# Nine matmuls into an unread PSUM bank, placed in TensorE's last waits for the values of a decode attention kernel

## The chip, the cores and the metric

The kernel runs on one core of a Trainium2 chip. The metric is the device time of one execution in microseconds, as the median of several. One execution per kernel is also recorded by the profiler; the profile's span is some 1.9 us shorter than the device time. The traces of before and after note 16 marks for each of the end's ten transfers, and the landing is taken as the last of them (value part 1 of before: 1264.21 to 1266.39 us); in before the matmuls that wait for one started 0.04 to 0.14 us after it.

## The reference

One token goes through a cached attention and a gated feed-forward; both are added to the input.

```python
xn = layernorm(x)                                      # x: (1, 1, 448)
q  = (xn @ wq).reshape(1, 1, 16, 256)                  # 16 query heads, 8 key/value heads
scores = einsum("bhqd,bhkd->bhqk", q, k) * 256**-0.5   # caches: (1, 8, 65536, 256), bf16
o  = einsum("bhqk,bhkd->bhqd", softmax(scores), v)
out = x + o.reshape(1, 1, 4096) @ wo + ffn(xn)         # ffn(xn) = xn + sigmoid(xn @ w_r) * gated feed-forward of xn
```

The two caches are 537 MB of the 549 MB that the kernel reads.

## The kernel before

The key and value blocks stream through three slots of SBUF. TensorE transposes keys, forms scores, and multiplies probabilities with values. Only the end matters here. The last value block (128 rows for each partition) arrives in six parts, so that little work is left after each landing; behind it, in the same queue of transfers, come the last pieces of the output weights.

```python
LAST = [64, 32, 16, 8, 4, 4]     # rows of the last value block in each part
DIRECT = 2                       # the last two parts are multiplied another way
...
slot_item("v", NT + 3, 2, [("last%d" % k if k < len(LAST) - 1 else "slot2", J) for k, J in enumerate(LAST)], [("SUM",)])
item("wx", [(wo_x, wo_rows(HL, HL + 1)[:, 0, FO // 2:FO, :]...)], [("HT",)])
ENDS = [(0, 0, NH), (1, 0, 1), (1, 1, NH)]
for k, (i, f0, f1) in enumerate(ENDS):
    item(("wo_end", k), [...])   # three more pieces of the output weights
```

The multiplication with the values, part by part. Four matmuls run side by side, each on a strip of 32 columns of the array (`tile_position=(0, 32 * g)`); in the trace of before the four of a group start within 0.01 us (part 1: 1266.530 to 1266.540):

```python
def pe_V(t, c, first, last, loose=False):
    ...
    for k, (_, J) in enumerate(parts):
        ...
        W_item("pe", ("v", t, k))                      # wait for the landing of part k
        def f(it, ...):
            if direct:                                 # parts 4 and 5: two moving columns each
                ...
            for j in range(lo, hi, 2):
                g = j // 2 % NG
                ins = mm(ps_o[32 * g:32 * g + 2 * rep, :],
                         lhsT=p_sb[:, c, j - c * CH:j - c * CH + 2, :]..., rhs=kv[:, j:j + 2, :],
                         start=..., stop=..., tile_position=(0, 32 * g), skip_group_check=loose)
            return ins
        O("pe", ("PV", t, c, k), f)
```

And what follows the values:

```python
values(NT + 3)               # the six parts
dve_ob(T); pe_oT(T)          # VectorE copies the sums out; TensorE regroups; VectorE normalises (OTSB)
W_item("pe", "wx")
O("pe", "FIN_X", fin_x)      # 4 matmuls of 224 columns
W("pe", "OTSB", T)
for k, (i, f0, f1) in enumerate(ENDS):
    W_item("pe", ("wo_end", k))
    O("pe", ("FIN", k), f)   # 4, then 2, then 2 matmuls of 224 columns
W("dve", "FIN", len(ENDS) - 1)
O("dve", "RESULT", ...)      # copy to bf16; two small transfers write it out
```

## Time and profile before

| | before |
|---|---|
| time, median of three runs | 1277.72 us (1277.71 to 1278.37) |
| span of the profiled run | 1275.8 us |
| read from HBM | 549.03 MB at 430 GB/s |
| TensorE matmul busy | 956.0 us, 75% |
| mean granted TensorE clock | 0.897 |
| last landing to copy of the result (trace) | 0.501 us |

The prediction shows the page, the chain, TensorE's instructions and the stretches of the clock. In the trace of before the granted clock is 0.50 or 1.00 throughout, and it changes only at steps that lie a multiple of 3.41 us apart (near the end at 1241.22, 1254.88, 1261.70, 1265.12 and 1268.53); a window of the clock is here a stretch of 3.41 us between such steps. In the timelines below a line has start us, length us, engine, source line, operation, output and inputs, shapes, count, and in brackets the idle time before and what ended it. A timeline merges neighbours, so the length of a merged line includes the waits inside it.

### The profile page before, as it was taken

Reading aid. Unit: us, or ns where it says so; the run is one execution under the profiler, and the core shown is the slowest. Engines: PE = TensorE matmul, PEld = TensorE weight load, DVE = VectorE, ACT = ScalarE, POOL = GpSimd, SP = SyncE. Lnnn points to the kernel's source line nnn. Section 1 sums busy time; section 2 is a strip of 40 time slices with the busy share of each in tenths; the row PEclk is TensorE's granted clock in tenths of the full one; section 3 lists DMA queues with packets and bytes.
Section 4 is the critical chain, followed back from the end, with each engine's and each line's share of the span. In section 5 each row is a group of like instructions: output and inputs, shape, how many; then the busy total and the mean of one; then the engine's idle time right before and its main releaser. Section 6 shows DMA issues by size and latency. Waiting matters only on the chain.

```text
span 1275.8 us, 23503 instructions
## 1 busy us (share of the span) xinstructions
PE 956.0 (75%) x9735; PEld 624.7 (49%) x9735; DVE 570.3 (45%) x1078; ACT 436.2 (34%) x655; POOL 8.0 (1%) x38
## 2 busy tenths in 40 slices
PE   3898988778777679767778776787777687677664
PEld 3676655445544455444455454454454454444321
DVE  4566554345444455343454344454444554444310
ACT  2455433244333334323333332343332333332300
POOL 2000000000000000000000000000000000000000
PEclk9899999899888899888898888898888998888886
DMA  9999999999999999999999999999999999999998
GB/s 408 426 429 443 432 436 432 434 432 438 434 429 438 427 440 429 436 436 429 438 432 436 432 434 427 440 432 434 438 427 438 432 436 434 432 432 436 426 431 353
DMA packets 12742, 549.20 MB, mean 430 GB/s; under 512 B 1335, under 2 KB 1978, under 8 KB 3386
## 3 DMA queue, kind: packets, MB, share of 16 engines
q1 hardware_dynamic: 12724, 549.03, 99.7%
q8 instruction: 8, 0.13, 0.0%
q14 instruction: 4, 0.03, 0.0%
q10 hardware_dynamic: 6, 0.00, 0.0%
HBM read 549.03 MB, written 0.00 MB: 430 GB/s over the span
## 4 chain that ended last, share of the span: by engine, by line
DMA 80%; PE 17%; issue 1%; ACT 1%; DVE 1%; SPq 0%; ACTq 0%; DVEq 0%
DMA ring<-in_A_v_cache_dram 68%; PE ps_o L420 12%; DMA ring<-in_A_k_cache_dram 7%; DMA kt_all<-in_A_wo_dram 3%; DMA ring<-in_A_wo_dram 2%; PE ps_t L420 2%; PE ps_q L420 1%; PE ps_m L420 1%; ACT kt_all L481 1%; SPq L910 0%; DVE kt_all L479 0%; ACT S_sb L562 0%; PE ps_s L420 0%; DVE kt_all L712 0%; DVE kt_all L815 0%
## 5 line engine op out<-in xcount | busy, mean ns | idle before, releaser
L420 PE MATMUL ps_t<-ident_f,ring 128*128 128x128 f32 x4096 | 586.6, 285 | 84.5 <-DMA ring<-in_A_k_cache_dram 61.6
L479 DVE COPY kt_all<-ps_t 128x1024 bf16<-128x1024 bf16 x768 | 487.0, 684 | 293.8 <-PE ps_q L420 289.0
L420 PEld LDWEIGHTS ps_t<-ident_f,ring 128*128 128x128 f32 x4096 | 450.2, 143 | 237.2 <-issue 135.2
L481 ACT ACTIVATE kt_all<-ps_t 128x1024 bf16<-128x1024 bf16 x256 | 262.0, 1023 | 508.4 <-PE ps_q L420 508.4
L420 PE MATMUL ps_o<-ring,p_sb 128*4 128x512 bf16 x2044 | 177.1, 508 | 204.6 <-DMA ring<-in_A_v_cache_dram 200.3
L420 PEld LDWEIGHTS ps_o<-ring,p_sb 128*4 128x4 bf16 x2044 | 53.0, 101 | 292.6 <-issue 264.2
L420 PE MATMUL ps_q<-kt_all,q_cur 128*2 128x512 bf16 x2056 | 164.9, 398 | 0.3 <-DVE kt_all L479 0.3
L503 ACT ACTIVATE s<-ps_q 98x512 bf16<-98x512 f32 x257 | 151.6, 590 | 1.3 <-PE ps_q L420 1.3
L585 DVE RECIPROCAL rs<-ps_m 128x4 f32<-128x4 f32 x29 | 5.3, 182 | 272.2 <-PE ps_m L420 272.2
L572 ACT ACTIVATE p_sb<-S_sb 128x128 bf16<-128x128 bf16 x64 | 18.9, 307 | 260.8 <-PE ps_o L420 260.6
L420 PEld LDWEIGHTS ps_s<-sel_bf,s 128*128 128x128 bf16 x1032 | 64.7, 98 | 5.3 <-ACT s L503 1.9
L420 PE MATMUL ps_s<-sel_bf,s 128*128 128x8 bf16 x1032 | 63.7, 167 | 1.3 <-ACT s L503 1.3
L628 DVE CAST ob_sb<-ps_o 100x512 bf16<-100x512 f32 x29 | 20.0, 691 | 89.9 <-PE ps_o L420 89.9
L420 PEld LDWEIGHTS ps_q<-kt_all,q_cur 128*2 128x2 bf16 x2056 | 26.4, 79 | 44.2 <-issue 44.2
L420 PEld LDWEIGHTS ps_m<-rowsum,ones_f 128*128 128x128 f32 x58 | 12.3, 264 | 22.6 <-issue 22.6
L481 ACT ACT_TABLE_LOAD x7 | 9.0, 1283 | 20.8 <-PE ps_q L420 20.8
L532 DVE TENSOR_REDUCE m1p<-S_sb (+1 forms) x33 | 13.9, 422 | 4.4
L420 PE MATMUL ps_m<-rowsum,ones_f 128*128 128x4 f32 x58 | 14.8, 326 | 0.0
L530 DVE CAST S_sb<-ps_s 128x256 f32 (+1 forms) x33 | 13.6, 413 | 1.9 <-PE ps_s L420 1.9
L562 ACT ACTIVATE S_sb<-S_sb,negmax 128x512 bf16<-128x512 bf16 x16 | 13.2, 851 | 3.2 <-DVE negmax L556 3.2
L420 PE MATMUL ps_m<-diag,ones_f 2*128 2x2 f32 x58 | 11.2, 260 | 3.6 <-DVE diag L547 0.6
L420 PEld LDWEIGHTS ps_m<-diag,ones_f 2*128 2x128 f32 x58 | 8.7, 187 | 10.5 <-DVE diag L547 10.5
(93 smaller groups left out, 128.3 us busy)
## 6 DMA issues: line engine op xcount, KB each, us to landing
ring<-in_A_k_cache_dram SPq DMA_DIRECT2D x8, 4096.0 KB, 30.5
ring<-in_A_v_cache_dram SPq DMA_DIRECT2D x1, 4096.0 KB, 27.3
ring<-in_A_wq_dram SPq DMA_DIRECT2D x1, 3584.0 KB, 11.5
ring<-in_A_wo_dram SPq DMA_DIRECT2D x1, 2688.0 KB, 28.7
ring<-in_A_v_cache_dram SPq DMA_DIRECT2D x1, 2048.0 KB, 31.8
ring<-in_B_w_gate_dram SPq DMA_DIRECT2D x1, 1568.0 KB, 16.5
ring<-in_B_w_up_dram SPq DMA_DIRECT2D x1, 1568.0 KB, 19.9
ring<-in_B_w_down_dram SPq DMA_DIRECT2D x1, 1568.0 KB
```

The source lines that it names most:

```text
L420: return pe.matmul(*a, **k)
L479: O(e, ("EV", s, m), lambda it: nc.vector.tensor_copy(out=kt[:, :], in_=tb[:, :]), f"ev{m}")
L481: O(e, ("EV", s, m), lambda it: nc.scalar.activation(out=kt[:, :], in_=tb[:, :], func=ACTF.Copy), f"ev{m}")
L503: O("act", ("EVQ", s), lambda it: nc.scalar.activation(out=s2[s % 2][0:QROWS, :], in_=ps_q[0:QROWS, :], func=ACTF.Copy), "evq")
L530: O("dve", ("SCOPY", u), lambda it: nc.vector.tensor_copy(out=S_sb[:, at(it, SBN), :], in_=ps_sn), "sc")
L532: O("dve", ("SMAX", u), lambda it: nc.vector.tensor_reduce(out=m1p[:, :, at(it, 1)], in_=S_sb[:, at(it, SBN), :].rearrange("p n i -> p i n ...
L562: O("act", ("EXP", h, i), lambda it, i=i: nc.scalar.activation(out=S_sb[:, :, i], in_=S_sb[:, :, i], func=ACTF.Exp, bias=negmax[:, i:i + 1 ...
L572: O("act", ("PC", t, c), lambda it: nc.scalar.activation(out=p_sb[:, c, :, :], in_=S_sb[:, n:n + CH, :], func=ACTF.Copy), "pc")
L585: O("dve", ("RS", t), lambda it: nc.vector.reciprocal(out=rs[:, :, :], in_=ps_m[0:P, C_TOT:C_TOT + NH * rep]))
L628: O("dve", ("OB", t), lambda it: nc.vector.tensor_copy(out=ob_sb[0:OROWS, :], in_=ps_o[0:OROWS, :]))
```

## The change

In the profile before, TensorE waits in the end for one small part after another, and its granted clock is at half (0.50) from 1268.53 us on. The change fills these waits with matmuls on stale data, and is meant to keep the clock up until the last steps. Their results go to a PSUM bank that nobody reads any more.

```diff
+WARM = {0: (5, 512), 1: (2, 512), 2: (1, 512), 3: (1, 256)}
...
             O("pe", ("PV", t, c, k), f)
+            if t == NT + 3 and k in WARM:
+
+                def keep(it, k=k):
+                    n_, cols = WARM[k]
+                    for _ in range(n_):
+                        ins = mm(ps_tf[3][0:2 * rep, 0:cols], lhsT=p_sb[:, c, 0:2, :].rearrange("p n i -> p (n i)"), rhs=slots[0][:, 0:cols],
+                                 start=True, stop=True, skip_group_check=True)
+                    return ins
+
+                O("pe", ("WARM", k), keep)
```

## The prediction

> **What bounds the kernel now.** I read the page first, then the chain that ended last, then TensorE's instructions of the last 15 us, then the trace's landing marks of the last transfers, and last the busy time cut along the granted clock's own steps. The page:
>
> ```profile
> PEclk9899999899888899888898888898888998888886
> DMA  9999999999999999999999999999999999999998
> ...
> DMA 80%; PE 17%; issue 1%; ACT 1%; DVE 1%; SPq 0%; ACTq 0%; DVEq 0%
> ```
>
> The DMA engines are busy at 90% or more in 39 of 40 slices and the kernel reads 549.03 MB at 430 GB/s, which is 1276.8 us against a span of 1275.8: the kernel is its transfers. The change leaves all of them as they are. Only what follows the last transfer can move. In the same page the clock row falls to 6 in the last slice, which is the mark that the change aims at. The chain that ended last, from the moment when the last transfers are queued:
>
> ```profile
> 1237.23 34.86 DMA kt_all<-in_A_wo_dram
> 1272.09 0.04 issue
> 1272.13 0.54 PE ps_s L420 x4
> 1272.67 0.08 issue
> 1272.74 0.93 PE ps_s L420 x8
> 1273.67 0.02 issue
> 1273.70 0.38 DVE kt_all L862
> ```
>
> On its face TensorE holds the end for 1.47 us (0.54 + 0.93) after a landing at 1272.09. Here are its instructions in the waits for the parts of the last value block (64, 32, 16, 8, 4, 4 rows) and after them:
>
> ```profile
> 1261.64 3.57 PE L420 MATMUL ps_o<-ring,p_sb 128*4 128x512 bf16 x32 [4.66 <-DMA ring<-in_A_v_cache_dram]
> 1266.53 1.03 PE L420 MATMUL ps_o<-ring,p_sb 128*4 128x512 bf16 x16 [1.32 <-DMA ring<-in_A_v_cache_dram]
> 1268.92 1.02 PE L420 MATMUL ps_o<-ring,p_sb 128*4 128x512 bf16 x8 [1.36 <-DMA ring<-in_A_v_cache_dram]
> 1270.21 0.60 PE L420 MATMUL ps_o<-ring,p_sb 128*4 128x512 bf16 x4 [0.26 <-DMA ring<-in_A_v_cache_dram]
> ```
>
> Sixteen matmuls took 1.03 us and then eight took 1.02: the clock fell between them. The aligned stretches show where (columns: stretch and length, then PE, PEld, DVE, ACT, POOL busy us with counts, granted clock, DMA share, GB/s):
>
> ```profile
> 1254.88:1258.29 3.41, 2.10 (x40) 0.72 (x32) 0.00 (x0) 0.62 (x2) 0.00 (x0) 1.00 1.00 428
> 1258.29:1261.70 3.41, 0.06 (x4) 0.09 (x8) 0.00 (x0) 0.00 (x0) 0.00 (x0) 1.00 0.96 408
> 1261.70:1265.12 3.42, 3.42 (x32) 0.95 (x31) 0.00 (x0) 0.00 (x0) 0.00 (x0) 0.50 0.95 402
> 1265.12:1268.53 3.41, 1.12 (x20) 0.32 (x16) 0.00 (x0) 0.00 (x0) 0.00 (x0) 1.00 0.99 403
> 1268.53:1271.94 3.41, 2.38 (x32) 0.88 (x32) 0.69 (x1) 0.00 (x0) 0.00 (x0) 0.50 0.92 336
> 1271.94:1275.36 3.42, 1.54 (x16) 0.38 (x13) 0.54 (x2) 0.00 (x0) 0.00 (x0) 0.50 0.05 15
> ```
>
> The clock of each stretch was decided by the stretch before: 3.42 us busy raised it, 2.10 us kept it, 1.12 and 0.06 us dropped it, and 2.38 us at the low clock did not raise it. So the whole end, from 1268.53 on, ran at half clock.
>
> The last step is the one that decides my number. The trace's landing marks (a transfer has landed with its sixteenth mark) stand at 1266.39, 1268.88, 1270.17, 1270.85 and 1271.51 for value parts 1 to 5, and at 1272.09, 1272.61, 1272.90 and 1273.20 for the four last pieces of the output weights. Each matmul group of the end starts at its own piece: the weight load of the last group is at 1273.24, 0.04 after the last landing. So the 1.47 us that the chain puts down to TensorE are nearly all waiting for four landings in a row; what TensorE alone owns is from 1273.24 to the end of the last pair of matmuls at 1273.65.
>
> [...]
>
> **The change part by part.** It adds nine matmuls of four weight columns: five of 512 after part 0, two of 512 after part 1, one of 512 after part 2, one of 256 after part 3. They write a score-transpose bank whose last reader was the FFN, so nobody waits for the result, and the vector engine's copy of the sums waits for part 3's own matmuls, ahead of the added one.
> - Cost of one, full clock: groups of four side by side start 0.215 us apart, and the added ones all use one column strip, so about 0.215 us each for 512 and 0.107 for 256. At half clock twice that.
> - After part 0: its last group starts at 1264.55 and streams 0.43 us at half clock, so the added five start near 1264.98; the clock rises at 1265.12; they stream until about 1266.12[...]. Part 1 lands at 1266.39. [...]
> - After part 1: its last group starts at 1267.18; two more end streaming near 1267.82; part 2 lands at 1268.88. No delay.
> - The stretch 1265.12 to 1268.53 now has 1.12 + some 1.0 + 0.43 = 2.6 us busy against 1.12, above the 2.10 that kept the clock. So it stays full past 1268.53. This is the step that I am surest of.
> - Part 2 then takes about 0.6 instead of 1.02 us, one added 0.215 us; part 3 about 0.38 instead of 0.60, one added 0.107 us, done near 1270.7; part 4 lands at 1270.85. No delay. The vector copy of 0.69 us starts some 0.2 us earlier, at about 1270.65.
> - Parts 4 and 5 and the regrouping are two-column matmuls [...]about 26 ns apart; they start at their landings and gain next to nothing.
> - The normalised sums (now ready at 1272.23) come perhaps 0.1 us earlier; the next matmul needs the piece of 1272.61. No gain.
> - The last pair: start held by the landing of 1273.20, so 1273.24 to 1273.26 either way. Its 391 ns (median of the eight 224-column matmuls) [...]if the clock is still full there.
>
> That last condition is open. Stretch 1268.53 to 1271.94 would hold about 0.60 + 0.22 + 0.38 + 0.11 = 1.3 us of wide matmuls and some 0.9 us of two-column ones. By busy time that is 2.2 us, on the side that keeps the clock; counting the wide ones alone it is 1.3, close to the 1.12 that lost it. I give it about an even chance, and in other executions the windows lie elsewhere. Sum: 0.13 us times about one half, 0.05 to 0.1 us off 1277.72.
>
> **Rivals.**
> 1. The chain at face value: 12 matmuls of 224 columns and the steps before them run at twice the rate, 0.5 to 0.8 us gained, time near 1277.0. For it: the chain names PE for 1.47 us and the clock is 0.50. Against: four landing marks inside that stretch.
> 2. The added matmuls run at half clock (other window position) and delay the next part: five take 2.13 us instead of 1.08, part 1 starts about 0.9 us late, and up to 0.4 us of this could reach the end; time near 1278.1. [...]Against: TensorE is busy without a break from 1261.64, so a full window lies behind it soon, and the waits later on (1.1 us before part 2) take up most.
> 3. The clock falls again at 1271.94: gain 0, time 1277.7.
> 4. TensorE's extra reads slow the transfers, which would count over the whole wait. Against: GB/s was 402 in the stretch with TensorE busy throughout and 408 in the idle one before it, no difference that tells.
>
> **Range and chances.** The three runs of before spread over 0.66 us (1277.71 to 1278.37), five times the gain that I expect, so the spread sets the range. Predicted 1277.6 us; 8 times in 10 between 1276.9 and 1278.6. A change of 2% would be 25 us, and everything after the last landing is about 2.6 us (1273.20 to 1275.8), so faster or slower by over 2% has half a percent each.
>
> **What would show it right or wrong.** Right: clock 1.00 past the window that ended at 1268.53 here, the eight matmuls of part 2 in about 0.6 us, unchanged landings, and the last pair still starting 0.04 to 0.06 us after the last landing[...]. Wrong: the matmuls on the last four pieces starting well before those landings (then rival 1), a part starting late after added matmuls (rival 2), or the last landing itself moved by more than 0.3 us, for which I know no reason.

Cut from it is what rested on figures that no trace or run of this case shows, or named none for them: a paragraph, the margin that it worked out for part 1, what paces the two-column matmuls, and the working of the only term in its sum with the length expected of the last pair. The sum came to 0.13 us at the last pair, if the clock is still full there, at about an even chance: 0.05 to 0.1 us off 1277.72. The 0.13 us was an estimate; the trace of after shows as much, with 0.257 to 0.258 us for a matmul of 224 columns at full clock (the four from 1271.95) against 0.391 to 0.394 at half (the last six, from 1272.71). What the forecast otherwise takes for the clock is in the trace of before: groups of 512 columns start 0.215 us apart at full clock (1266.53 to 1267.18) and 0.427 at half (1261.99 to 1264.55), one matmul of them is on record for 0.376 to 0.379 us there and 0.634 here, and two-column matmuls start 0.026 to 0.028 us apart (1270.94 to 1271.10); the 0.107 us for 256 columns is half of 0.215, an estimate. That the stretch before decides the clock is my reading of the six stretches printed there. That the windows lie elsewhere in other executions had not been shown then; the later traces show it (one began at 1265.12 us in before, 1265.47 in after, 1265.03 in warm_end).

## The result, and the profile after

| | before | after |
|---|---|---|
| time, median of six runs each | 1277.72 us (1277.18 to 1278.37) | 1277.53 us (1277.47 to 1279.52) |
| span of the profiled run | 1275.8 us | 1275.6 us |
| mean granted clock | 0.897 | 0.882 |
| last landing (trace) | 1273.20 us | 1273.02 us |
| last landing to copy of the result | 0.501 us | 0.499 us |

The ratio is 1.0001, with a 95% interval of 0.9988 to 1.0013: the same. It is not the ratio of the medians: the means of these runs, the late one of 1279.52 included, are 1277.85 and 1277.78 us. The mean granted clock is that of the whole span; it was 0.882 to 0.893 in the six runs of the changed kernel, and says nothing of the end.

TensorE in the waits, kernel after:

```profile
1264.28 1.84 PE L421 MATMUL ps_t<-ring,p_sb 128*4 128x512 bf16 x5
1266.37 1.03 PE L421 MATMUL ps_o<-ring,p_sb 128*4 128x512 bf16 x16 [0.25 <-DMA ring<-in_A_v_cache_dram]
1267.23 0.59 PE L421 MATMUL ps_t<-ring,p_sb 128*4 128x512 bf16 x2
1268.78 0.60 PE L421 MATMUL ps_o<-ring,p_sb 128*4 128x512 bf16 x8 [0.95 <-DMA ring<-in_A_v_cache_dram]
...
1270.07 0.39 PE L421 MATMUL ps_o<-ring,p_sb 128*4 128x512 bf16 x4 [0.48 <-DMA ring<-in_A_v_cache_dram]
...
1271.95 0.36 PE L421 MATMUL ps_s<-kt_all,oT_h 128*1 128x224 bf16 x4
1272.57 0.91 PE L421 MATMUL ps_s<-kt_all,oT_sb 128*1 128x224 bf16 x8 [0.26 <-DMA kt_all<-in_A_wo_dram]
```

The added matmuls are the lines with `ps_t`. The eight matmuls of part 2 take 0.60 us where they took 1.02, part 3 takes 0.39 for 0.60, and the first four output matmuls 0.36 for 0.54: the change does to TensorE what it was written for. The last eight still take 0.91 us. The clock's stretches say why (columns as in the prediction: stretch, length, PE, PEld, DVE, ACT, POOL busy with counts, clock, DMA share, GB/s):

```profile
1265.47:1268.89 3.42, 2.22 (x25) 0.68 (x27) 0.00 (x0) 0.00 (x0) 0.00 (x0) 1.00 0.99 401
1268.89:1272.30 3.41, 2.33 (x38) 0.90 (x30) 0.85 (x2) 0.00 (x0) 0.00 (x0) 1.00 0.83 303
1272.30:1275.60 3.30, 0.92 (x10) 0.28 (x8) 0.38 (x1) 0.00 (x0) 0.00 (x0) 0.50 0.01 4
```

The stretch with part 1 now kept the clock (it lost it before), so the next was full to 1272.30; that one lost it, 0.27 us before the last eight matmuls. The chain that ended last, kernel after:

```profile
1238.99 33.44 DMA kt_all<-in_A_wo_dram
1272.43 0.14 issue
1272.57 0.93 PE ps_s L421 x8
```

It now leaves the transfers at the landing of the second weight piece (1272.43) instead of the first (1272.09): the four matmuls between are no longer long enough to be on it. In both kernels the two later pieces land inside the 0.93 us: at 1272.74 and 1273.02 after. The span is 0.2 us shorter because the last landing was 0.17 us earlier in this execution; from there to the copy the two kernels differ by 0.002 us.

### The profile page after: what moved, and what is told of

It is laid out like the page before. It is cut to its first block, busy times and chain, and to the rows that moved or that the text cites. A ratio compares the mean times of both kernels' runs of the same rounds, so it can differ in the third digit from the quotient of the medians.

```text
span 1275.6 us, 23521 instructions
## 1 busy us (share of the span) xinstructions
PE 963.0 (75%) x9744; PEld 629.2 (49%) x9744; DVE 570.8 (45%) x1078; ACT 436.6 (34%) x655; POOL 8.1 (1%) x38
## 3 DMA queue, kind: packets, MB, share of 16 engines
q1 hardware_dynamic: 12724, 549.03, 99.7%
HBM read 549.03 MB, written 0.00 MB: 430 GB/s over the span
## 4 chain that ended last, share of the span: by engine, by line
DMA 80%; PE 17%; issue 1%; ACT 1%; SPq 1%; DVE 1%; ACTq 0%; DVEq 0%
DMA ring<-in_A_v_cache_dram 68%; PE ps_o L421 12%; DMA ring<-in_A_k_cache_dram 7%; DMA kt_all<-in_A_wo_dram 3%; DMA ring<-in_A_wo_dram 2%; PE ps_t L421 2%; PE ps_q L421 1%; PE ps_m L421 1%; ACT kt_all L482 1%; SPq L921 1%; DVE kt_all L480 0%; ACT S_sb L563 0%; DVE kt_all L723 0%; PE ps_s L421 0%; DVE kt_all L826 0%
```

## The experiments

My theory: the end hangs on the landings of the last four weight pieces, and a full clock is worth about 0.13 us there (0.391 us of a matmul less the 0.258 in after), if it lasts to the last pair of matmuls. Its main rival: the 1.47 us that the chain gave to TensorE are TensorE's own. Below, "last gap" is the time from the last landing to the copy of the result. Twelve experiments ran, seven with new kernels and five with the two unaltered ones again. All gave correct results. Where a ratio is given, it is to the kernel before, timed in the same rounds.

| kernel | time us, median | last gap us |
|---|---|---|
| before; plain1, plain2 (the same again) | 1277.72; 1277.41, 1277.44 | 0.501; 0.504, 0.511 |
| after; again1, again2, again3 (the same again) | 1277.53; 1277.49, 1277.06, 1277.50 | 0.499; 0.347, 0.348, 0.517 |
| warm_end | 1277.43 | 0.346 |
| weights_first | 1279.03 | 1.783 |
| weights_first_warm | 1279.08 | 1.412 |
| dose10 | 1277.45 | 0.508 |
| dose30 | 1280.28 | 3.277 |
| narrow | 1278.54 | 0.495 |
| strips40 | 1277.27 | 0.347 |

From the start of the copy to the end of the span it is 2.04 to 2.06 us in every one of them.

### warm_end: enough added matmuls to keep the clock to the last pair

```diff
-WARM = {0: (5, 512), 1: (2, 512), 2: (1, 512), 3: (1, 256)}
+WARM = {0: (5, 512), 1: (4, 512), 2: (3, 512), 3: (2, 512), 4: (1, 512)}
...
         O("pe", "FIN_X", fin_x)
+        O("pe", "WARM_X", lambda it: mm(ps_tf[3][0:2 * rep, 0:512], ...))   # one more of 512 columns
```

> More added matmuls (5, 4, 3, 2, 1 of 512 columns after parts 0 to 4, and one between the first of the last four weight pieces and the second), so that the clock is full until the last pair. My theory (the end hangs on the four landings): the last pair still starts within 0.07 us of the last landing, takes 0.26 in place of 0.39 us; from the last landing to the start of the result's copy 0.33 to 0.38 us in place of 0.50 before; time 1277.4, ratio 0.9997 to 1.0002. Rival (the chain's 1.47 us of TensorE is TensorE's own): 0.5 to 0.8 us faster than the kernel before.

The clock was full through the end (stretches of warm_end):

```profile
1268.45:1271.86 3.41, 3.02 (x38) 1.25 (x38) 0.69 (x1) 0.00 (x0) 0.00 (x0) 1.00 0.95 350
1271.86:1275.27 3.41, 1.32 (x14) 0.46 (x13) 0.54 (x2) 0.00 (x0) 0.00 (x0) 1.00 0.06 19
```

The last pair started 0.04 us after the last landing, and the last gap is 0.346 us: 0.155 us less than before. Median 1277.43 against 1277.57 of its rounds, ratio 0.9998 (0.9984 to 1.0012). The rival's 0.5 to 0.8 us are not in the last gap. With the clock full to the end more filling has nothing left to gain here, and the times can't tell this kernel from the one before.

### weights_first: no landing between the last steps

```diff
-    slot_item("v", NT + 3, 2, [...LAST...], [("SUM",)])
-    item("wx", [...], [("HT",)])
+    item("wx", [...], [("HT",), ("SUM",)])
     for k, (i, f0, f1) in enumerate(ENDS):
         item(("wo_end", k), [...])
+    slot_item("v", NT + 3, 2, [...LAST...], [("SUM",)])
```

> The kernel before without added matmuls, the four last weight pieces queued ahead of the last value parts, so that the last landing is a value part and no landing stands between the last steps. My theory: the whole of the end becomes TensorE's and VectorE's own, from the last landing to the copy of the result about 1.9 us at half clock in place of 0.50, so 1.3 to 1.5 us slower (1279.0). Rival (the end was TensorE's own already): the same time as before, within 0.3 us.

The kernel before with the other order took 1279.03 us, 1.46 us more than the 1277.57 of its rounds (ratio 1.0012, interval 0.9999 to 1.0026, so the times alone just fail to show it). The trace does: its last landing is 0.12 us later than before, and its last gap of 1.783 us now is TensorE's and VectorE's own. The chain of weights_first:

```profile
1249.02 24.30 DMA ring<-in_A_v_cache_dram
1273.32 0.05 issue
1273.37 0.48 PE ps_m L420 x12
1273.85 1.23 PE ps_s L420 x7
1275.08 0.02 issue
1275.10 0.38 DVE kt_all L862
```

So in the kernel before this work did lie beside transfers, and the order of the queue hides some 1.3 us of it. The 1.47 us that the chain of before gives to TensorE are not idle waiting: its twelve output matmuls took 1.28 us here (1273.78 to 1275.06) with no landing between them. But they start at one landing after another, and only what follows the last one counts. The rival falls.

### weights_first_warm: the same order with a full clock

The edit is weights_first's order on the changed kernel, with `WARM = {0: (5, 512), 1: (4, 512), 2: (3, 512), 3: (2, 512), 4: (1, 512)}`.

> The same order of transfers, with 5, 4, 3, 2, 1 added matmuls after parts 0 to 4. My theory: where no landing stands between the last steps the clock does pay: if full to the end, from the last landing to the copy of the result about 1.3 us against 1.9 in weights_first, so 0.5 to 0.6 us faster than weights_first and still 0.8 us slower than before. Rival: faster than the kernel before by 0.5 us.

The last gap fell to 1.412 us, by 0.37 us: the clock pays once TensorE owns the end, some 2.4 times what it paid in warm_end. It is less than the 0.5 to 0.6 that I expected, and the chain of weights_first_warm shows one reason:

```profile
1271.23 0.60 PE ps_o L421 x8
1271.83 0.64 PE ps_t L421 x3
1272.47 0.35 PE ps_o L421 x4
1272.82 0.42 PE ps_t L421 x2
1273.24 0.28 PE ps_m L421 x8
1273.53 0.31 PE ps_t L421
1273.83 0.39 PE ps_m L421 x12
1274.22 0.82 PE ps_s L421 x12
```

The added matmuls (`ps_t`) had come onto the path. Parts 2 and 3 still started at their landings (0.04 us after), but parts 4 and 5 stood behind added ones and started 0.15 and 0.11 us after theirs (1273.02 and 1273.65); part 5 of weights_first started after 0.05. That is some 0.06 us of the last gap. Its time, 1279.08, does not differ from that of weights_first: its last landing was 0.33 us later in the profiled execution, and the runs of either kernel spread over some 2 us. How much the times would show is left open; the rival's half microsecond below the kernel before does not appear, as the median is 1.5 us above it.

### dose10 and dose30: what an overrun costs

```diff
-WARM = {0: (5, 512), 1: (2, 512), 2: (1, 512), 3: (1, 256)}
+WARM = {0: (10, 512), 1: (2, 512), 2: (1, 512), 3: (1, 256)}     # dose10
+WARM = {0: (30, 512), 1: (2, 512), 2: (1, 512), 3: (1, 256)}     # dose30
```

> Ten instead of five added matmuls after part 0. They need about 2.2 to 3.2 us where the wait is about 1.4, so part 1 starts 0.9 to 1.5 us after its landing. My theory: the later waits (1.0 to 1.3 us before part 2, 0.5 before part 3) take it up; last landing to copy of the result as in the changed kernel (0.4 to 0.5 us), time 1277.5. Rival (added matmuls that overrun a wait cost their overrun): 1 us slower, 1278.6.

> Thirty instead of five after part 0: about 6.7 us of matmuls from some 1264.5, so they run 4.9 us past the landing of part 1, to about 1271.2. My theory: the waits from there on hold some 3 us of slack; after those 30 there remain 4 + 2 + 2 + 1 + 1 rounds of 0.215 us, the 0.7 us vector copy, regrouping and the last weights at full clock, so the last pair ends near 1275.0 in place of 1273.5: 1.0 to 2.2 us slower than before (1279.3). Rival (every added matmul costs its 0.215 us): 25 x 0.215 = 5.4 us slower, 1283.

dose10: 1277.45 us, ratio 0.9997 (0.9981 to 1.0014), last gap 0.508. The overrun after part 0 is taken up by the later waits, as expected: part 2 started 0.05 us after its landing. The overrun was smaller than the 0.9 to 1.5 us expected: part 1 landed at 1266.11, its first matmuls started at 1266.29, and those behind the added ones, by the spacing of the records, at 1266.93. dose30: 1280.28 us against 1277.75 of its rounds, ratio 1.0016 (0.9999 to 1.0033; each of its four runs is slower than each of the seven of before), last gap 3.277: 2.8 us lost there, 2.5 in the medians, where I expected 1.0 to 2.2 and the rival 5.4. The mechanism holds and the size was off. From the first added matmul on, the added ones' strip has 40.5 rounds of 512 columns to do: 30, then 4 + 2 + 2 + 1 + 1 and a half. In this execution the clock was half until 1266.68, so the rounds between 1265.15 and 1266.68 took 0.43 us each (3.6 rounds), and the other 36.9 took 0.2157 us, 7.96 us: 1274.64. The strip's last matmul of 256 columns started at 1274.55. I had taken full clock throughout and a start 0.65 us earlier.

dose10 brought something that I had not expected. Its timeline:

```profile
1265.63 1.03 PE L421 MATMUL ps_t<-ring,p_sb 128*4 128x512 bf16 x4
1266.29 0.39 PE L421 MATMUL ps_o<-ring,p_sb 128*4 128x512 bf16 x3
1266.49 0.38 PE L421 MATMUL ps_t<-ring,p_sb 128*4 128x512 bf16 x1
1266.50 0.39 PE L421 MATMUL ps_o<-ring,p_sb 128*4 128x512 bf16 x3
1266.71 0.38 PE L421 MATMUL ps_t<-ring,p_sb 128*4 128x512 bf16 x1
1266.72 1.24 PE L421 MATMUL ps_o<-ring,p_sb 128*4 128x512 bf16 x10
```

Part 1's matmuls (`ps_o`) start in threes ahead of the last two added ones, which stand before them in the program. My reading is that the three are on the strips that the added matmuls leave free, and that those of the first strip follow at the back; the trace does not name strips, so the next experiment tests it.

### strips40: is that an order for each column strip?

```diff
-WARM = {0: (5, 512), ...}
+WARM = {0: (40, 512), ...}
...
-                    for _ in range(n_):
-                        ins = mm(ps_tf[3][0:2 * rep, 0:cols], ...
+                    for n in range(n_):
+                        g = n % NG if k == 0 else 0
+                        ins = mm(ps_tf[3][32 * g:32 * g + 2 * rep, 0:cols], ..., tile_position=(0, 32 * g), ...
```

> Forty added matmuls after part 0, dealt over the four column strips, so ten on each strip in place of dose10's ten on one. In dose10 twelve matmuls of part 1 on the other three strips started at its landing, ahead of two added ones that stand before them in the program. If each strip has an order of its own, here no matmul of part 1 can start before the tenth added one of its strip has streamed: the first starts some 0.4 to 0.9 us after the landing of part 1, the last ends as in dose10 (about 1.5 us after that landing). If the starts in dose10 were only mislabelled records, part 1 starts as in dose10. Time 1277.6, no different from the changed kernel.

Of the twelve, the lines of dose10 above show six ahead of an added one, three for each of the last two; that they are on the other strips was my reading.

With all four strips occupied none of part 1's matmuls got ahead (timeline of strips40):

```profile
1264.73 3.59 PE L421 MATMUL ps_t<-ring,p_sb 128*4 128x512 bf16 x40
1268.15 1.03 PE L421 MATMUL ps_o<-ring,p_sb 128*4 128x512 bf16 x16
```

They started at 1268.15, 2.0 us after the landing of part 1 at 1266.12. I had expected 0.4 to 0.9: the clock was half until 1267.28 here, so the ten groups took longer, and part 1 ended later than in dose10. The point in question is answered for these two runs: the order bound within a strip (none of part 1 before 1268.15 here) and not across strips (in dose10 matmuls of part 1 at 1266.29 and 1266.50, ahead of added ones at 1266.49 and 1266.71). Even so the last gap is 0.347 us.

### narrow: what keeps the clock, time in flight or columns?

```diff
-WARM = {0: (5, 512), 1: (2, 512), 2: (1, 512), 3: (1, 256)}
+WARM = {0: (40, 2), 1: (16, 2), 2: (8, 2), 3: (4, 2)}
```

> The same counts of busy time in place of the nine wide matmuls, but of two columns each (40, 16, 8, 4 after parts 0 to 3). If the clock follows any instruction in flight, the stretch after part 0 and 1 has some 2.4 us of matmuls on record and the clock stays full past it. If it follows columns that stream, the stretch holds only the 0.9 us of part 1 and the clock falls, as in the kernel before. I expect the second. Time either way 1277.5 within 0.5 us.

The stretch with part 1, kernel narrow, and the one after it:

```profile
1265.55:1268.96 3.41, 2.71 (x80) 1.92 (x72) 0.00 (x0) 0.00 (x0) 0.00 (x0) 1.00 0.99 402
1268.96:1272.37 3.41, 2.23 (x32) 1.07 (x32) 0.62 (x1) 0.00 (x0) 0.00 (x0) 0.50 0.91 328
```

2.71 us of matmuls on record, more than the 2.22 that kept the clock in the changed kernel, and the clock fell. I then estimated the time in which columns stream, as a share of the full-clock stretch, overlaps counted once. The rate is from the traces: at half clock groups of 512 columns start 0.427 us apart (before, from 1261.99 to 1264.55), which is 1.2 columns a ns, and at full clock I took twice that; the 0.216 us measured there (before, seven steps from 1255.08 to 1256.59) give 1% less:

| stretch | busy us | columns streaming | clock in the next |
|---|---|---|---|
| before, 1254.88 | 2.10 | 57% | full |
| before, 1265.12 | 1.12 | 25% | half |
| after, 1265.47 | 2.22 | 55% | full |
| after, 1268.89 | 2.33 | 31% | half |
| narrow, 1265.55 | 2.71 | 37% | half |
| warm_end, 1268.45 | 3.02 | 57% | full |

Busy time does not order these rows and streaming columns do. The same count over all full-clock stretches from 1250 us on, in all fourteen profiles, agrees: the 22 that kept the clock had shares of 42% and more (busy time from 1.62 us), the 24 that lost it 37% and less (busy time up to 2.71 us). This holds for the end of the kernel only: stretches of the main loop, made mostly of transposes, kept the clock at a share of 25% by this count (before, from 125.06), so it is no rule for them. The time of narrow (1278.54, one run) is later than the 1277.0 to 1278.0 that I expected by 0.5 us; its last landing was at 1274.04, the latest of all, and its last gap is as before.

### again1 to again3 and plain1, plain2: other positions of the windows

These are the changed kernel and the kernel before, unaltered.

> The changed kernel once more, unaltered, to see another position of the clock's windows. My theory: the clock is full past the window that holds part 1, and from the last landing to the copy of the result it is 0.35 to 0.37 us if the clock is still full at the last pair and 0.50 if not, and nothing else. Rival (a window position can make the added matmuls delay the end): above 0.55.

> As again1: 0.35 to 0.37 us or 0.50 us from the last landing to the copy of the result; about an even chance of each. Rival: above 0.55.

> As again1: 0.35 to 0.37 us or 0.50 us from the last landing to the copy of the result; about an even chance of each. Rival: above 0.55.

> The kernel before once more, unaltered, for another position of the clock's windows. My theory (without the added matmuls the waits drop the clock wherever the windows lie): half clock at the last pair, 0.49 to 0.52 us from the last landing to the copy of the result. Rival (the kernel before reaches the end at full clock as often as the changed one, and its one profile was an unlucky position): 0.35 us in about half of such looks.

> As plain1: 0.49 to 0.52 us from the last landing to the copy of the result. Rival: 0.35 us in about half of such looks.

The changed kernel's last gap was 0.347, 0.348 and 0.517 us, with the 0.499 of its first profile two of four at full clock. The kernel before stayed at 0.504 and 0.511. So the changed kernel does reach the last pair at full clock, in some executions. The mean of the four is 0.428 us against 0.505 of the three of before: 0.08 us, from few profiles. What decided was where the clock's windows of 3.41 us lay. In all four the clock, once it had risen for the last time, was full for two windows and then fell: at 1272.30 and 1272.17 (the first profile and again3), before the last pair, and at 1273.47 and 1273.89 (again1 and again2), after it.

This leaves one rival open. The windows of the three profiles of before began 0.4 to 1.3 us ahead of the landing of part 1, as in the first profile and again3 (0.8), which gained nothing; again1 and again2, where one began 0.3 and 1.2 us after it, have no counterpart among them. That the kernel before would be at half clock there too is likely (an estimate from before's timeline gives some 2 us of busy time in the half-clock window that would have to raise it, and 2.38 did not raise the clock in before from 1268.53, nor 2.60 in weights_first from 1269.39, while 2.97 did in before from 1251.46), but not shown. For the filling itself warm_end is the fair comparison: its window began at 1265.03, 1.2 us ahead of part 1, as in plain1 (1265.02, 1.1 us), and its last gap was 0.346 against 0.504.

No gap came near a delay. Yet a window position can make the added matmuls overrun, and it did so in the two profiles that gained. In again1, where the clock was half until 1266.65, the fifth added one began after part 1 had landed (1266.35), and part 1's three free strips went ahead of it; in again2, with half clock until 1267.06, it began 0.31 us after that landing. The lines of again1, with the last output matmuls (0.74 us in place of 0.91):

```profile
1266.48 0.44 PE L421 MATMUL ps_o<-ring,p_sb 128*4 128x512 bf16 x3
1266.65 0.38 PE L421 MATMUL ps_t<-ring,p_sb 128*4 128x512 bf16 x1
...
1272.69 0.74 PE L421 MATMUL ps_s<-kt_all,oT_sb 128*1 128x224 bf16 x8 [0.26 <-DMA kt_all<-in_A_wo_dram]
```

## Why the prediction was right

- **The kernel is its transfers, and the end hangs on the last four landings.** Right. In the unaltered kernels and in warm_end, narrow, dose10 and strips40 the last pair started 0.04 to 0.08 us after the last landing; with the landings moved out of the way the last gap went from 0.50 to 1.78 us. Two of its steps prove less than they say. 549.03 MB at 430 GB/s is the span over again, as 430 is the mean over the span; the DMA row carries that point. And "nearly all waiting" is too much: 0.47 us of the 1.47 follow the last landing (1273.20 to 1273.67), and the rest is work that lies beside transfers.
- **The stretch with part 1 keeps the clock.** Right in all four profiles of the changed kernel, though in again2 part 1 began at half clock; in all three of before the last pair ran at half clock (last gap 0.501 to 0.511 us). My reason was wrong: I compared busy times (2.6, measured 2.22, against 2.10 and 1.12), and narrow shows that busy time is not what counts.
- **No part is delayed.** Right in the first profile, with 0.1 us to spare (the fifth added matmul ended at 1266.12, part 1 landed at 1266.24). In again1 and again2 it was wrong: rival 2 began to happen, and the later waits took it up, as they did in dose10 with ten.
- **0.13 us at the last pair, at an even chance.** The gain measured 0.15 us (0.501 to 0.347 and 0.348) and came in two of four profiles, but not for the reason that I weighed. Of my two ways of reading the stretch from 1268.53, busy time, "on the side that keeps the clock", failed: that second window lost the clock in all four (busy 1.8 to 2.4 us). The gain came where the second window ended after the last pair; I had only named that the windows lie elsewhere in other executions. That two of four came out is luck. **Rival 3**, no gain as the clock falls before the last pair, is what happened in the first profile and in again3.
- **Rival 1**, the chain at face value, fell with warm_end and weights_first. **Rival 4**, slower transfers, has nothing for it: with the wait filled the transfers ran at 401 GB/s (after, 1265.47 to 1268.89) against 403 in the stretch of before.
- **1277.6 us, 1276.9 to 1278.6.** Measured 1277.53. That it is so close is luck: this execution gained nothing at the end (0.499 against 0.501 us). The 0.19 us between the medians is not shown to be the change's: the last landing alone moved between 1272.70 and 1273.20 us over the seven profiles of the two unaltered kernels.

## What to carry to other kernels

Before paying for a faster step on the chain, look at the landing marks inside it: a group of matmuls that starts at one landing after another is put down to TensorE, but a faster clock here only shortened what follows the last landing (from 0.50 to 0.35 us). Filling the waits kept TensorE's clock here only where the filler streamed columns (55% of the stretch in after kept it, 37% in narrow did not), and cost nothing only as long as later waits took up its overrun (none lost with dose10, 2.8 us with dose30), so count both ends of the budget at half clock, and look at more than one profile, as the windows of the clock lay elsewhere in each (the last one of full clock ended at 1272.30, 1273.47, 1273.89 and 1272.17 us in the four of the changed kernel). And where the order of the last transfers can be chosen, that choice (1.3 us of the last gap here) may be worth far more than the clock (0.15 us).
